# Token windows of 224 instead of 256 in the expert stage, with another order of routing, gap and dense entry, in a fused attention, expert and dense kernel

## The chip, the cores and the metric

The kernel runs on one core of one Trainium2 chip. The metric is the device time of one execution in microseconds (us), the median of three runs. The engines are TensorE (PE; its weight loads stand apart as PEld), VectorE (DVE), ScalarE (ACT), GpSimd (POOL) and SyncE (SP, which issues most DMAs). Each engine works off its own queue in order, and engines wait for one another by semaphores.

## The reference

Three stages on 1,536 tokens, cut to what matters:

```python
# A: attention, B=2, H=8, S=768, D=64; a key is seen only in its query's hash bucket
mask   = q_bucket[:, :, :, None] == k_bucket[:, :, None, :]      # 6 sign bits of x @ proj
attn   = softmax(where(mask, q @ k.T / 8, -1e9))
x      = (attn @ v) as (1536, 512)
# B: one expert of 8 for each token, w1[e] 512x1024, w2[e] 1024x512, capacity 384
expert = argmax(x @ w_gate);  gate_w = softmax(x @ w_gate)[expert]
disp[e, pos] = x[i]           # pos counts the tokens of expert e so far
y      = relu(disp @ w1) @ w2;  out[i] = gate_w[i] * y[expert[i], pos[i]]
# C: dense block, w_in 512x2048, w_out 2048x512
h = out @ w_in;  g = h * clip(h + 3, 0, 6) / 6;  result = g @ w_out
```

With the inputs that the reference draws, the eight experts get 192, 202, 210, 177, 218, 182, 193 and 162 tokens.

## The kernel before

All large products are made of operands that are split in two: a high part that TensorE takes in its faster fp32 form (`fp32r`), and the rest. ACT copies the high part, DVE or Pool subtracts it, and a product takes three matmuls (high by high, low by high, high by low). Weight tiles are `wh` and `wl` (experts), `ia`/`ib` and `ch`/`cl` (dense block); activations are `xh`/`xl`, `hh`/`hl`, `yTh`/`yTl`, `gh`/`gl`.

**Attention (stage A)** runs over 96 steps, one for each chunk of 128 queries of a head. In a step PE makes scores, transposes and the product with v, ACT evicts (`pf`, L398) and takes the high part (`phi`, L406), DVE reduces, and Pool makes the low part (`plo`, L412) of most steps. Work beside the steps (preparing heads, gating, routing) is put into a queue by `at(step, f)` and `spread(step, generator, distance)`, which runs one piece of a generator, up to its next `yield`, every `distance` steps; `due` (called twice a step) issues what has fallen due. The numbers in the table `Q` are such places; `Q['ht']` is a count of dummy matmuls, called heats, which only keep PE busy.

**Routing.** `route(b, ...)` takes the gate logits `lg` of half b of the tokens and finds expert, place in the expert (`pos`) and, by comparing with `edges`, the window in which the token lies. `rh` and `rg` carry token number and gate weight into a matrix of places (`ohr`), and `windows` sums them by matmuls into `ids` (which token stands at a place) and `gates`. `weigh(b)` makes the gate weights. Half 0 is done within the attention; half 1 only after its last step: that stretch, from the last attention step to the first expert product, is called the gap here.

**The gap** goes: rest of `route(1)`, `ids`, `gather(0)` (two indirect DMAs on Pool's queue fetch two tiles `xg` of 128 tokens), the rest of the gate weights, `gates`, `scale_x` (DVE multiplies `xg` by the gate), `make_x` (PE transposes the tiles, ACT and DVE split them into `xh`, `xl`), first `gemm1`. Beside it the first expert's `w1` is split by `split_w(wp, e, i, q, lo)`: tile i of the expert in four quarters q of 512 columns, ACT for `wh` (L131), and DVE or Pool for `wl` (L132). Before the change the four quarters of the first half and three of the second have Pool as `lo`.

**Experts (stage B).** An expert's window of W = 256 tokens is the moving side of all its matmuls, the weights (128 x 128) are the stationary side:

```python
for l, r in ((a, xh), (b, xh), (a, xl)):      # gemm1, 8 tiles of 128 hidden units
    for k in range(KD):                       # KD = 4
        pe.matmul(ps, l[:, c], r[:, k], ...)  # 128x128 weights, W columns
```

`gemm1` (L953) makes 96 matmuls and `gemm2` (L970) makes 96, so eight experts make 1,536. The splits of the next weights, the loads, the next gather and the transposes of its tiles are written between them. The result goes to `yTh`/`yTl` at the expert's offset. During the last expert's second product the dense block's weights begin to be loaded and decoded.

**Overflow.** Tokens of an expert behind the window (W to 384) are done by `rest(e)` under a branch, `If(over > 0)`, which loads the expert's weights once more.

**Dense block (stage C).** The weights come as 64-bit words. `decode` (L999, L1002, L1003) makes fp32 of one 128 x 512 tile in three DVE operations; `split_in` and `halve` split it on ACT (`ia`, `ch`) and Pool (`ib`, `cl`). The loop runs over 32 blocks m (16 groups of hidden units for each half of 768 tokens): `up(m)` makes a group's hidden values (24 matmuls, L1209, in two pieces of 512 and 256 tokens; ACT L1211 and DVE L1212 evict each, then ACT L1221 and DVE L1222 split), and `down(m - 2)` makes 18 matmuls (L1231). `dec_c` decodes the next tile; from m = 2 on it is also called inside `up`, between the two pieces. Behind the branch ten matmuls on `warm_ps` (L1195) come first.

Of the kernel before, what the change touches and what calls it, by code (L numbers as in the profile page):

```python
# [33 lines left out]
W = 256  # L34
CB = 768
NS = NT // P
YW = NT + W
# [12 lines left out]
def moe_attention_kernel(ctx, tc, qk, v, vt, pj, wg, w1, w2, win, wout, out, cap):  # L50
# [27 lines left out]
    edges = persist([P, 4], F32, "edges")  # L78
# [7 lines left out]
    ids = persist([P, E, 3], I32, "ids")  # L86
    gates = persist([P, E, 3], F32, "gates")
# [6 lines left out]
    def consts():  # L94
# [9 lines left out]
        pool.iota(edges, pattern=[[P, 4]], base=0, channel_multiplier=0, **small)  # L104
# [47 lines left out]
    jo = rtile([B, NC, 3], "jo")  # L152
    rh = rtile([B, NC, E, 3], "rh", F16)
    rg = rtile([B, NC, E, 6], "rg", F16)
# [9 lines left out]
    def route(b, psum):  # L164
# [23 lines left out]
        for i in range(b):  # L188
# [7 lines left out]
        ge = rtile([n, 4], f"ge{b}")  # L196
        dve.tensor_tensor(out=ge, in0=bc(pos[:, b], 4), in1=mid(edges, n), op=ALU.is_ge)
        yield
        dve.tensor_tensor(out=t1, in0=ge[:, :, 1], in1=ge[:, :, 2], op=ALU.add)
        dve.tensor_tensor(out=jo[:, b], in0=ge[:, :, 0:3], in1=ge[:, :, 1:4], op=ALU.subtract)  # L200
        yield
        place = rtile([n], f"pl{b}")
        dve.scalar_tensor_tensor(out=place, in0=t1, scalar=-float(P), in1=pos[:, b], op0=ALU.mult, op1=ALU.add)
        jt = rtile([n, 3], f"jt{b}")
        dve.scalar_tensor_tensor(
            out=jt, in0=bc(tokid[:, b * n : (b + 1) * n], 3), scalar=1.0, in1=jo[:, b], op0=ALU.add, op1=ALU.mult
# [4 lines left out]
        for c in range(n):  # L211
            if b and c == n - 1:
                off = rtile([P], "off")
                act.activation(off, iota_r, AF.Square, bias=place[:, c : c + 1], scale=-1.0)
                act.activation(ohr[:, b, c], off, AF.Relu, bias=1.0, scale=-1.0)
                continue
            dve.tensor_scalar(
                out=ohr[:, b, c], in0=iota_r, scalar1=place[:, c : c + 1], scalar2=None, op0=ALU.is_equal
            )

    def weigh(b):
# [13 lines left out]
        jt = rtile([n, 3], f"jg{b}")  # L235
        dve.tensor_tensor(out=jt, in0=jo[:, b], in1=bc(gt[:, b], 3), op=ALU.mult)
        j2 = rtile([n, 6], f"j2{b}", F16)
        dve.tensor_copy(j2[:, :, 0:3], jt)
        yield
        dve.tensor_tensor(out=jt, in0=jt, in1=j2[:, :, 0:3], op=ALU.subtract)  # L240
        dve.tensor_scalar(out=j2[:, :, 3:6], in0=jt, scalar1=LS, scalar2=None, op0=ALU.mult)
# [13 lines left out]
    Q = {'v': (-3.25, -4.75, -1.75, -2.25), 'vg': (-4.5, -4.75), 'vgd': 1, 'pr': (-13.0, -12.75, -12.0, -12.5), 'prd': 0.6, 'b0': 7.75, 'b': 1.75, 'bd': 0.5, 'vm0': (8.0, 8.25, 10.75, 13.0), 'vm': (-0.5, 4.75, 7.0, 12.25), 'vs': 13.25, 'pa': 1.5, 'ev': 0.5, 'lvt': -5.0, 'v4': (2.0, 3.75, 4.0, 16.25), 'vg0': (1.85, -4.4, 7.75), 'p2': 3.5, 'lr': (0, 3, 1.5, 4.5), 'lv': 5.5, 'vsd': 0.75, 'ac': (0, 0, 2, 6, 7, 8, 9, 10), 'hd': (3, 5, 17), 'hn': (4, 4, 2, 2, 4, 3, 0, 0, 0), 'ap': (0,), 'h0': (7,), 'hl': (4,), 'l0': (), 'll': (1, 10), 'ht': (4, 4)}  # L255


    with ExitStack() as actx:
# [524 lines left out]
        for q in range(4):  # L783
            split_w(wp1, 0, 0, q, pool)
# [16 lines left out]
        for _ in range(7):  # L801
            next(rgen)

# [126 lines left out]
    def make_x(e, j):  # L930
# [7 lines left out]
        c = slice(j * P, (j + 1) * P)  # L938
# [95 lines left out]
    dve.tensor_copy(ids, ps1[:, : 3 * E].rearrange("p (e j) -> p e j", e=E))  # L1034
# [9 lines left out]
    ps2 = ps2[:, : 6 * E].rearrange("p (e j) -> p e j", e=E)  # L1044
    dve.tensor_copy(gates, ps2[:, :, 0:3])
    dve.scalar_tensor_tensor(
        out=gates, in0=ps2[:, :, 3:6], scalar=1.0 / LS, in1=gates, op0=ALU.mult, op1=ALU.add
    )
# [74 lines left out]
    with ExitStack() as octx:  # L1123
# [14 lines left out]
        def rest(e):  # L1138
            ra = act.value_load(offs[0:1, E + e : E + e + 1], min_val=0, max_val=NT)
            rv = dve.value_load(offs[0:1, E + e : E + e + 1], min_val=0, max_val=NT)  # L1140
            t = op.tile([P, DM], F32, tag="xo", name=f"xo{e}")
            pool.indirect_dma_start(
                out=t, out_offset=None, in_=xd,
                in_offset=bass.IndirectOffsetOnAxis(ap=ids[:, e, 2:3], axis=0),
            )
            dve.tensor_scalar(out=t, in0=t, scalar1=gates[:, e, 2:3], scalar2=None, op0=ALU.mult)
            ps = pso.tile([P, KD, P], F32, tag="a", name=f"psoa{e}")
            for k in range(KD):
                pe.transpose(ps[:, k], t[:, k * P : (k + 1) * P], ident)
            xo = op.tile([P, KD, P], F32, tag="xt", name=f"xot{e}")  # L1150
            act.activation(xo, ps, AF.Copy)
            ho = op.tile([P, KF, P], F32, tag="ho", name=f"ho{e}")
            for i in range(2):
# [170 lines left out]
```

## Time and profile before

| | us |
|---|---|
| median of three runs | 740.39 |
| the three runs | 734.89, 740.39, 741.52 |
| the profiled execution | 734.49 |
| its span | 732.8 |
| its time outside the span | 1.7 |

| engine | busy us of the span | share |
|---|---|---|
| PE | 695.7 | 95% |
| PEld (weight loads) | 617.5 | 84% |
| DVE | 508.6 | 69% |
| ACT | 383.7 | 52% |
| POOL | 267.1 | 36% |

Matmuls are pipelined and their ends are modelled, so the distance between starts tells what a matmul costs, and not its duration. The granted TensorE clock is given as a share of full speed (2.4 GHz); 0.5 is the lower level (1.2 GHz). The trace shows how the span divides: attention to 228, its last steps and the gap to 259.2, experts to 451.8, the branch to 457.1, and the dense block to the end.

### The profile page before, as it was taken

To read this page: it belongs to the slowest core of one execution; us is meant where nothing else is said; L and a number is where in the kernel's file an instruction comes from. 1 tells how busy PE (TensorE), PEld (TensorE's weight loads), DVE (VectorE), ACT (ScalarE), POOL (GpSimd) and SP (SyncE) were. 2 spreads that over 40 slices of the span, in tenths; PEclk is the share of its full clock that TensorE was granted. 3 is DMA by queue.
4 is the path that set the end of the run, shared out by engine and by line. 5 is a ranking of instruction groups with operands and counts; after the bars stand their busy time and mean duration, and the time that the engine had idled before them with its cause. 6 is when DMAs were issued, how large, how long until landed. Compare 5 with 4: busy or idle time off the path is not lost. (4 is left out here: it accounts for less than half of the span.)

```text
span 732.8 us, 14199 instructions
## 1 busy us (share of the span) xinstructions
PE 695.7 (95%) x5518; PEld 617.5 (84%) x5518; DVE 508.6 (69%) x981; ACT 383.7 (52%) x713; POOL 267.1 (36%) x208
## 2 busy tenths in 40 slices
PE   7999999999889399999999998899999999999996
PEld 2589898899878299999999997788888788888885
DVE  6779888987988867778777777788888732222320
ACT  2468788788769355556555662333333433332320
POOL 4366987887762711100110002333333423221112
PEclk9899999999989789999999999999999999999999
DMA  7576847745460466666666553234433001000001
GB/s 218 135 202 158 241 112 178 229 120 135 127 171 24 125 201 205 194 195 201 198 201 193 172 184 120 82 120 129 129 115 119 27 15 44 30 0 1 1 29 58
DMA packets 37839, 94.14 MB, mean 128 GB/s; under 512 B 7576, under 2 KB 13720, under 8 KB 37760
## 3 DMA queue, kind: packets, MB, share of 16 engines
q1 hardware_dynamic: 34672, 85.71, 39.9%
q0 software_dynamic: 2400, 7.36, 3.0%
q8 instruction: 47, 0.77, 0.4%
q14 instruction: 32, 0.26, 0.1%
q10 hardware_dynamic: 688, 0.03, 0.1%
HBM read 67.14 MB, written 6.29 MB: 100 GB/s over the span
## 5 line engine op out<-in xcount | busy, mean ns | idle before, releaser
L412 POOL TENSOR_TENSOR plo<-pf,phi 128x768 f16<-128x768 f32 x86 | 146.6, 1732 | 62.5 <-ACT phi L406 22.0
L988 POOL TENSOR_TENSOR ib<-wi,ia 128x512 fp32r<-128x512 f32 x32 | 49.1, 1535 | 192.5 <-ACT ia L987 189.4
L382 DVE TENSOR_REDUCE mx<-psm 128x1 f32<-128x384 f32 x192 | 96.4, 549 | 28.2 <-PE psm L379 28.1
L398 ACT ACTIVATE pf<-pst 128x384 f32<-128x384 f32 x192 | 84.1, 488 | 51.5 <-PE pst L397 47.9
L132 DVE TENSOR_TENSOR wl<-raw,wh 128x512 fp32r<-128x512 f32 x121 | 86.4, 724 | 8.1 <-ACT wh L131 2.8
L1209 PE MATMUL psg<-yTh,ia 128*128 128x512 f32 (+1 forms) x256 | 86.9, 339 | 3.5 <-DVE rl L1212 3.1
L1212 DVE SCALAR_TENSOR_TENSOR rl<-rl,psg 128x512 f32<-128x512 f32 x64 | 35.1, 551 | 73.7 <-ACT rl L1211 73.7
L1209 PE MATMUL psg<-yTl,ia 128*128 128x512 f32 (+1 forms) x256 | 86.1, 336 | 0.0
L1209 PE MATMUL psg<-yTh,ib 128*128 128x512 f32 (+1 forms) x256 | 86.1, 336 | 0.0
L1211 ACT ACTIVATE rl<-psg,b 128x512 f32<-128x512 f32 x64 | 37.0, 580 | 84.9 <-PE psg L1209 80.9
L131 ACT ACTIVATE wh<-raw 128x512 fp32r<-128x512 f32 x128 | 77.0, 623 | 2.0 <-issue 2.0
L396 PE MATMUL pst<-Y,K 128*128 128x384 f32 x192 | 75.3, 392 | 0.0
L1231 PE MATMUL pso<-ch,gh 128*128 128x512 f32 x192 | 75.0, 391 | 0.0
L1231 PE MATMUL pso<-ch,gl 128*128 128x512 f32 x192 | 75.0, 391 | 0.0
L1231 PE MATMUL pso<-cl,gh 128*128 128x512 f32 x192 | 74.7, 389 | 0.0
L970 PE MATMUL psy<-hh,wh 128*128 128x256 f32 x256 | 73.7, 288 | 0.0
L406 ACT ACTIVATE phi<-pf 128x768 f16<-128x768 f32 x85 | 71.7, 844 | 2.0
L379 PE MATMUL psm<-K,X 76*128 76x384 f32 x192 | 68.3, 434 | 4.4 <-DVE mx L382 2.2
L970 PE MATMUL psy<-hl,wh 128*128 128x256 f32 x256 | 72.4, 283 | 0.0
L970 PE MATMUL psy<-hh,wl 128*128 128x256 f32 x256 | 72.4, 283 | 0.0
L424 PE MATMUL psv<-vh,phi 128*128 128x73 f16 x576 | 70.2, 200 | 0.0
L425 PE MATMUL psv<-vh,phi 128*128 128x72 f16 x576 | 69.7, 201 | 0.0
(204 smaller groups left out, 1681.0 us busy)
## 6 DMA issues: line engine op xcount, KB each, us to landing
raw<-in_w_dram SPq DMA_DIRECT2D x64, 512.0 KB
rc<-in_win_dram SPq DMA_DIRECT2D x16, 512.0 KB
rc<-in_wout_dram SPq DMA_DIRECT2D x16, 512.0 KB
r<-in_qk_dram SPq DMA_DIRECT2D x16, 384.0 KB
K<-hi SPq DMA_DIRECT2D x31, 192.0 KB
vr<-in_v_dram SPq DMA_DIRECT2D x4, 768.0 KB
vt<-in_vt_dram SPq DMA_DIRECT2D x8, 384.0 KB
Y<-hi SPq DMA_DIRECT2D x16, 192.0 KB
```

Of the source, the lines that this page charges most:

```text
L131: act.activation(wh[e, i][:, c], r, AF.Copy)
L132: lo.tensor_tensor(out=wl[e, i][:, c], in0=r, in1=f32(wh[e, i])[:, c], op=ALU.subtract)
L382: dve.tensor_reduce(out=mm[:, c, n : n + 1], in_=ps[:, :HS], axis=AX.X, op=ALU.max)
L396: pe.matmul(ps[:, :HS], st["K1"][:, kc], st["Y"][:, qc], start=True, stop=False)
L398: act.activation(pf.rearrange("k (c n p) -> k c n p", c=NC, n=2)[:, :, n], ps[:, :HS].rearrange("k (p c) -> k c p", c=NC), AF.Exp, scale=0 ...
L406: act.activation(phi_t[k], pf_t[k], AF.Copy)
L412: eng.tensor_tensor(out=plo_t[k], in0=pf_t.pop(k), in1=phi_t[k], op=ALU.subtract)
L424: pe.matmul(o, hi[:, cc], vv[:, j, 0:VA], start=j == 0 and c == 0, stop=False, **grp)
L425: pe.matmul(o[:, 0:DE], hi[:, cc], vv[:, j, VA:VW], start=False, stop=False, **grp)
L970: pe.matmul(ps, l, r, start=n == 0, stop=n == 3 * KF - 1)
L1209: pe.matmul(ps, l, x, start=n == 0, stop=n == 3 * KD - 1)
L1231: pe.matmul(po[blk][s], l, r, start=first and n == 0, stop=last and n == 2)
```

## The change

1. **Width.** A window is GW = 112 tokens instead of 128, so W = 224 instead of 256, and there are NW = 4 windows up to the capacity instead of 3. `edges`, `jo`, `rh`, `rg`, `ids` and `gates` grow accordingly, and `rest` loops over two windows. Gathers and transposes still take 128 tokens; `make_x` evicts 112 columns.
2. **Routing.** `route` has a further `yield` after `rs`, and one ahead of each column for half 0; it begins at step 66 with a distance of 1.5 (before: 70 and 1), `weigh(0)` at 84 (before: 88). One more piece of `route(1)` is issued ahead of the gap's code.
3. **Gap.** The first half of the first `w1` is split within attention steps 88.5 to 94.5, by ACT and DVE. Of the second half two quarters are split ahead of `scale_x` and two behind `make_x`, by DVE. Pool makes none of them. The loads of the first `w2` are issued behind `make_x`. Heats: 2 new ones, then 5 and 9 in place of 4 and 4.
4. **Dense entry.** `warm_ps` is allocated ahead of the branch from the pool `pso` that is open there, with 12 matmuls instead of 10. From m = 1 on, the loop issues `up(m)` first, then `split_in(m + 2)` and `dec_c`.

```diff
-W = 256
+GW = 112
+W = 2 * GW
+NW = 4
@@ route
+        yield
         ps = psum()
...
-        dve.tensor_tensor(out=t1, in0=ge[:, :, 1], in1=ge[:, :, 2], op=ALU.add)
+        dve.tensor_reduce(out=t1, in_=ge[:, :, 1:NW], axis=AX.X, op=ALU.add)
...
         for c in range(n):
+            if not b:
+                yield
@@ attention
-        spread(70, route(0, lambda: misc("psr0")))
-        spread(88, weigh(0))
+        spread(66, route(0, lambda: misc("psr0")), 1.5)
+        spread(84, weigh(0))
         for i in range(4):
             at(NC * (NH - 3) + i, load_w, 0, i // 2, i % 2)
+            at(STEPS - 7.5 + 2 * i, split_w, wp1, 0, 0, i)
@@ end of attention
-        for q in range(4):
-            split_w(wp1, 0, 0, q, pool)
...
-        for _ in range(7):
+        for _ in range(8):
             next(rgen)
+        heat(ps_t, "t", 2)
@@ make_x
-        c = slice(j * P, (j + 1) * P)
+        c = slice(j * GW, (j + 1) * GW)
+        ps = ps[:, :, 0:GW]
@@ gap
     gather(0)
     heat(HT[0])
-    for q in range(3):
-        split_w(wp1, 0, 1, q, pool)
     run(wgen)
-    for q in range(4):
-        load_w(0, 2 + q // 2, q % 2)
     windows(ps2, ohr, rg, [B - 1])
...
-    split_w(wp1, 0, 1, 3)
+    split_w(wp1, 0, 1, 0)
+    split_w(wp1, 0, 1, 1)
     for j in range(2):
         scale_x(0, j)
     for j in range(2):
         make_x(0, j)
+    for q in range(2, 4):
+        split_w(wp1, 0, 1, q)
+    for q in range(4):
+        load_w(0, 2 + q // 2, q % 2)
@@ ahead of the branch / dense entry
+        warm_ps = pso.tile([P, 512], F32, tag="w", name="warm_ps", bufs=1)
         with tc.If(over > 0):
...
+        for _ in range(12):
+            pe.matmul(warm_ps, ident16, mid(ident16, 4), start=True, stop=True)
...
-        warm_ps = ps_g.tile([P, 512], F32, tag="g", name="warm_ps")
-        for _ in range(10):
-            pe.matmul(warm_ps, ident16, mid(ident16, 4), start=True, stop=True)
@@ dense loop
-            if m + 2 < TOT:
-                split_in(m + 2)
-            dec_c()
+            if m == 0:
+                split_in(2)
+                dec_c()
             if m < TOT:
                 up(m)
+            if 0 < m < TOT - 2:
+                split_in(m + 2)
+            if m > 0:
+                dec_c()
```

**DVE in the gap, around the gates.** Each row is an instruction: line, operation, written tile, read tiles, shape; numbers behind a name are buffer numbers, `wl0_1` is the second half of the first expert's w1. Before:

```order
L1046 SCALAR_TENSOR_TENSOR gates_77<-psg_4973,gates_77 128x24
L132 TENSOR_TENSOR wl0_1_5022<-raw0_1_1_3895,wh0_1_5021 128x512
L928 TENSOR_SCALAR xg00_5013<-xg00_5013,gates_77 128x512
L928 TENSOR_SCALAR xg01_5015<-xg01_5015,gates_77 128x512
L940 TENSOR_TENSOR xl0_5065<-psa00_5066,xh0_5064 128x4x128
```

DVE had one `wl` here, behind the gates; Pool made the three other quarters. The same place after:

```order
L1049 SCALAR_TENSOR_TENSOR gates_77<-psg_4977,gates_77 128x32
L135 TENSOR_TENSOR wl0_1_5055<-raw0_1_0_3849,wh0_1_5054 128x512 x2
L934 TENSOR_SCALAR xg00_5017<-xg00_5017,gates_77 128x512
L934 TENSOR_SCALAR xg01_5019<-xg01_5019,gates_77 128x512
L947 TENSOR_TENSOR xl0_5063<-psa00_5064,xh0_5062 128x4x112
L947 TENSOR_TENSOR xl0_5063<-psa01_5071,xh0_5062 128x4x112
L135 TENSOR_TENSOR wl0_1_5055<-raw0_1_1_3890,wh0_1_5054 128x512 x2
```

All four quarters stand on DVE now, two ahead of the scalings and two behind the evictions of the transposes.

**ACT in the last attention steps.** `wh_0` is the first expert's w1. Before, the copies of its first half follow the last step (the first of the two rows of four):

```order
L398 ACTIVATE pf_4406<-pst_4407 128x6x64
L398 ACTIVATE pf_4406<-pst_4411 128x6x64
L406 ACTIVATE phi_4435<-pf_4406 128x768
L131 ACTIVATE wh_0_4514<-raw_0_0_3761 128x512 x2
L131 ACTIVATE wh_0_4514<-raw_0_1_3809 128x512 x2
```

After, they stand among the steps; this is the last of them:

```order
L404 ACTIVATE pf_4382<-pst_4383 128x6x64
L404 ACTIVATE pf_4382<-pst_4387 128x6x64
L134 ACTIVATE wh_0_4196<-raw_0_1_3808 128x512
L412 ACTIVATE phi_4415<-pf_4382 128x768
```

One copy stands ahead of a step's `phi`, and nothing but the step's own work is left behind the last one.

**DVE at the dense entry, from the end of block 0 on.** `rl1` and `gl1` are block 1's evictions, `wi4` is the decoding of tile 4. Before:

```order
L1222 TENSOR_TENSOR gl0_9151<-rl0_9119,gh0_9150 128x768
L999 TENSOR_SCALAR wi4_9162<-rc4_0_7705 128x512
L1002 SCALAR_TENSOR_TENSOR wi4_9162<-rc4_0_7705,wi4_9162 128x512
L1003 SCALAR_TENSOR_TENSOR wi4_9162<-rc4_0_7705,wi4_9162 128x512
L1212 SCALAR_TENSOR_TENSOR rl1_9168<-rl1_9168,psg10_9169 128x512
L1212 SCALAR_TENSOR_TENSOR rl1_9168<-rl1_9168,psg11_9184 128x256
```

After:

```order
L1233 TENSOR_TENSOR gl0_10051<-rl0_10019,gh0_10050 128x768
L1223 SCALAR_TENSOR_TENSOR rl1_10054<-rl1_10054,psg10_10055 128x512
L1223 SCALAR_TENSOR_TENSOR rl1_10054<-rl1_10054,psg11_10070 128x256
L1233 TENSOR_TENSOR gl1_10086<-rl1_10054,gh1_10085 128x768
L1006 TENSOR_SCALAR wi4_10097<-rc4_0_7715 128x512
L1009 SCALAR_TENSOR_TENSOR wi4_10097<-rc4_0_7715,wi4_10097 128x512
```

The decoding moved behind block 1's evictions.

## Rows read from the trace of the kernel before

**Rows 1.** Windows: stretch, length, busy us (count) by engine, granted clock, DMA share, GB/s.

```profile
0.00:228.00 228.00, 215.45 (x2307) 184.39 (x2308) 188.09 (x431) 164.01 (x296) 156.85 (x122) 0.96 0.61 163
228.00:259.20 31.20, 19.07 (x254) 13.79 (x252) 25.50 (x64) 18.12 (x39) 16.92 (x15) 0.83 0.34 106
259.20:451.80 192.60, 192.58 (x1606) 192.05 (x1606) 148.09 (x301) 109.32 (x231) 14.33 (x14) 0.99 0.60 187
457.10:580.00 122.90, 119.62 (x608) 101.47 (x608) 105.42 (x128) 44.74 (x74) 41.90 (x29) 1.00 0.34 107
```

**Rows 2.** Waits of PE from 225 to 560: total us, times, longest.

```profile
PE psa L937 <- DVE xg L928: 4.2, 1, 4.2
PE warm_ps L1195 <- ACTq L1176: 3.0, 1, 3.0
PE psg L1209 <- DVE rl L1212: 2.7, 1, 2.7
```

**Rows 3.** Timeline of PE: start, us, operation, written<-read, stationary, output, count.

```profile
52.46 1.49 PE L485 MATMUL psg<-wg_sb,vt 128*128 128x16 f32 x12
53.79 0.43 PE L396 MATMUL pst<-Y,K 128*128 128x384 f32 x1
```

**Rows 4.** Weight loads by line: busy us, mean ns, idle time before them.

```profile
L970 PEld LDWEIGHTS psy<-hh,wl 128*128 128x128 f32 x256 | 49.0, 191 | 0.0
...
L485 PEld LDWEIGHTS psg<-wg_sb,vt 128*128 128x128 f32 x96 | 11.9, 198 | 0.0
```

**Rows 5.** Windows as in rows 1, three short stretches.

```profile
229.50:238.50 9.00, 8.97 (x148) 7.42 (x147) 7.65 (x19) 8.84 (x17) 1.55 (x1) 1.00 0.02 4
259.20:262.00 2.80, 2.80 (x13) 2.71 (x14) 1.33 (x2) 0.45 (x1) 1.25 (x2) 0.50 0.94 287
442.30:452.50 10.20, 9.48 (x80) 9.28 (x78) 9.93 (x16) 2.81 (x6) 3.61 (x2) 1.00 0.43 129
```

**Rows 6.** Timeline of ACT at the end of the attention, columns as in rows 3.

```profile
238.41 2.17 ACT L131 ACTIVATE wh<-raw 128x512 fp32r<-128x512 f32 x4
```

**Rows 7.** Timeline of POOL in the gap.

```profile
239.86 4.93 POOL L132 TENSOR_TENSOR wl<-raw,wh 128x512 fp32r<-128x512 f32 x4
250.83 0.97 POOL L921 DMA_INDIRECT xg<-xd,ids  x1 [0.30 <-DVE rg L160]
251.81 3.71 POOL L132 TENSOR_TENSOR wl<-raw,wh 128x512 fp32r<-128x512 f32 x3
```

**Rows 8.** Timeline of DVE in the gap.

```profile
241.36 1.05 DVE L461 TENSOR_TENSOR lg<-xp,lg 128x48 f32<-128x48 f32 x1
242.68 0.95 DVE L172 TENSOR_TENSOR dl<-lg,mx 128x48 f32<-128x48 f32 x1
243.66 1.19 DVE L175 SCALAR_TENSOR_TENSOR sc<-dl,rank 128x48 f32<-128x48 f32 x1
245.12 0.21 DVE L180 TENSOR_TENSOR oh<-sc,mx 128x48 f16<-128x48 f32 x1
...
251.31 4.77 DVE L132 TENSOR_TENSOR wl<-raw,wh 128x512 fp32r<-128x512 f32 x1
256.00 0.87 DVE L928 TENSOR_SCALAR xg<-xg,gates 128x512 f32<-128x512 f32 x2
259.77 0.76 DVE L132 TENSOR_TENSOR wl<-raw,wh 128x512 fp32r<-128x512 f32 x1
```

**Rows 9.** Transfers of the gathered tiles, 240 to 300, from the view of that tile.

```profile
DMA to landing us min/median/max: 3.3/4.1/6.1
```

**Rows 10.** The chain that ended last: start, us, engine, tile, line.

```profile
464.07 1.44 DVE wi L999
465.53 1.65 DVE wi L1002
...
579.24 0.42 DVE rl L1212
...
581.40 4.11 PE pso L1231 x18
```

More of the change, by code (lines that the diff above doesn't have):

```diff
@@ L33 @@
 KG = DF // P
-W = 256
+GW = 112
+W = 2 * GW
+NW = 4
 CB = 768
 NS = NT // P
-YW = NT + W
+YW = NT + 2 * P
 DE = D + E
@@ L85, in moe_attention_kernel @@
     lg = persist([P, B, NC, E], F32, "lg")
-    ids = persist([P, E, 3], I32, "ids")
-    gates = persist([P, E, 3], F32, "gates")
+    ids = persist([P, E, NW], I32, "ids")
+    gates = persist([P, E, NW], F32, "gates")
     inv = persist([P, NS], I32, "inv")
@@ L103, in consts @@
         pool.iota(iota_r, pattern=[[1, P]], base=0, channel_multiplier=0, **small)
-        pool.iota(edges, pattern=[[P, 4]], base=0, channel_multiplier=0, **small)
+        pool.iota(edges, pattern=[[GW, NW + 1]], base=0, channel_multiplier=0, **small)
+        pool.memset(edges[:, NW:], float(cap))
         pool.iota(iota_s, pattern=[[1, NS]], base=0, channel_multiplier=0, **small)
@@ L233, in weigh @@
         yield
[L235 to L238, printed above, removed]
+        jt = rtile([n, NW], f"jg{b}")
+        dve.tensor_tensor(out=jt, in0=jo[:, b], in1=bc(gt[:, b], NW), op=ALU.mult)
+        j2 = rtile([n, 2 * NW], f"j2{b}", F16)
+        dve.tensor_copy(j2[:, :, 0:NW], jt)
         yield
-        dve.tensor_tensor(out=jt, in0=jt, in1=j2[:, :, 0:3], op=ALU.subtract)
-        dve.tensor_scalar(out=j2[:, :, 3:6], in0=jt, scalar1=LS, scalar2=None, op0=ALU.mult)
+        dve.tensor_tensor(out=jt, in0=jt, in1=j2[:, :, 0:NW], op=ALU.subtract)
+        dve.tensor_scalar(out=j2[:, :, NW:], in0=jt, scalar1=LS, scalar2=None, op0=ALU.mult)
         yield
@@ L1033, in moe_attention_kernel @@
     windows(ps1, ohr, rh, [B - 1])
-    dve.tensor_copy(ids, ps1[:, : 3 * E].rearrange("p (e j) -> p e j", e=E))
+    dve.tensor_copy(ids, ps1[:, : NW * E].rearrange("p (e j) -> p e j", e=E))
     gather(0)
     heat(HT[0])
-    for q in range(3):
-        split_w(wp1, 0, 1, q, pool)
     run(wgen)
-    for q in range(4):
-        load_w(0, 2 + q // 2, q % 2)
     windows(ps2, ohr, rg, [B - 1])
     heat(HT[1])
-    ps2 = ps2[:, : 6 * E].rearrange("p (e j) -> p e j", e=E)
-    dve.tensor_copy(gates, ps2[:, :, 0:3])
+    ps2 = ps2[:, : 2 * NW * E].rearrange("p (e j) -> p e j", e=E)
+    dve.tensor_copy(gates, ps2[:, :, 0:NW])
     dve.scalar_tensor_tensor(
-        out=gates, in0=ps2[:, :, 3:6], scalar=1.0 / LS, in1=gates, op0=ALU.mult, op1=ALU.add
+        out=gates, in0=ps2[:, :, NW:], scalar=1.0 / LS, in1=gates, op0=ALU.mult, op1=ALU.add
     )
-    split_w(wp1, 0, 1, 3)
+    split_w(wp1, 0, 1, 0)
+    split_w(wp1, 0, 1, 1)
     for j in range(2):
@@ L1140, in rest @@
             rv = dve.value_load(offs[0:1, E + e : E + e + 1], min_val=0, max_val=NT)
[L1141 to L1153, printed above, removed]
-                r = op.tile([P, 2048], F32, tag="wo", name=f"wo{e}{i}", bufs=2)
-                sp.dma_start(out=r, in_=w1[e, :, i * 2048 : (i + 1) * 2048])
-                for f in range(4):
-                    ps = pso.tile([P, P], F32, tag="h", name=f"psoh{e}{i}{f}")
-                    for k in range(KD):
-                        pe.matmul(
-                            ps, r[:, k * 512 + f * P : k * 512 + (f + 1) * P], xo[:, k],
-                            start=k == 0, stop=k == KD - 1,
-                        )
-                    act.activation(ho[:, 4 * i + f], ps, AF.Relu)
```

69 lines of the change are left out of this document (47 added, 22 removed).

## The prediction

> **What bounds the kernel now.** I read the windows by stage first. In the attention TensorE is busy for 215.45 of 228 us, in the expert stage for 192.58 of 192.60 us at a granted clock of 0.99, and in the first half of the dense block for 119.62 of 122.9 us [rows 1]. Only the stretch from 228 to 259.2 us is different: 19.07 of 31.2 us, at 0.83. So a change that makes matmuls shorter is worth its full amount in the expert stage, and a change in the order of instructions is worth something only in the gap and at the dense block's entry, where TensorE waits. Next I read TensorE's waits from 225 to 560 us [rows 2]: 4.2 us for the scaled tiles `xg`, 3.0 us of `warm_ps` for ACT, 2.7 us for a dense eviction on DVE. These waits and the clock are all that parts 2 to 4 of the change can win. The sum below is made against the profiled execution: 734.49 us, a span of 732.8 and 1.7 outside. That execution lies 5.9 us under the median of 740.39; two runs lie at 734.5 to 734.9, two at 740.4 to 741.5. A measurement of this kernel can therefore hardly tell 1% (7.4 us) from no change.
>
> **The width: −13.0 us (bounds 0 and −19.4).** In the expert stage 1,606 matmuls take 192.58 us [rows 1], which is 119.9 ns each; 1,536 of them are the expert products, 184 us. What would a matmul of 224 columns take? Two things can pace it. One is the columns. A dense matmul of 512 columns takes 4.11 / 18 = 228 ns [rows 10], one of 256 takes 120, so a column costs (228 − 120) / 256 = 0.42 ns, and 224 columns would take 120 − 32 × 0.42 = 106.5 ns. The other is the load of its 128 x 128 fp32 weights, which every product needs anew and which the width doesn't shorten. The nearest row for that are the gate matmuls: they have only 16 columns, with loads of the same form, and twelve of them take from 52.46 to 53.79 us [rows 3], 111 ns each. Their loads last 198 ns in the mean, and the experts' 191 [rows 4], so a load of split weights is not seen to be slower than theirs. I take 111 ns: 9 ns gained on each. The bounds are 106.5 ns (the columns, were the load quicker than in the gate) and 120 ns (no row excludes that the experts' loads already pace their matmuls). The last expert's second product, 96 matmuls, is left out of the count, because there DVE is busy for 9.93 of 10.2 us with evictions and four decodings [rows 5] and sets the end. So 1,440 × 9 ns = 13.0 us, and 1,440 × 13.5 = 19.4 at most.
>
> The Trainium skill (TensorE: Matmul & The Clock Gate, section LDWEIGHTS) speaks against the hope that width pays in full: it gives a load as its columns divided by 1.2 GHz, whatever the contraction, so an estimate from that page is 107 ns for 128 columns and a gain of 13 ns each, 18.7 us in all. By the gate's 111 ns the trace agrees within 4 ns; no row has these products under 256 columns.
>
> Other work is no new bound there: DVE has 148.09 and ACT 109.32 us of 192.6 [rows 1], their evictions get shorter with the width, and the DMA share of 0.60 would rise to 0.64 in 179 us. The wider `ids`, `gates` and `rh` and the new places of `route(0)` and `weigh(0)` I count at zero: in the attention DVE has 40 us free [rows 1], and 0.5 us either way changes no bound.
>
> **The gap: −4.2 us (bounds −0.4 and −6.9).** Four terms.
>
> (a) The four `wh` copies of the first half take 2.17 us together [rows 6]. They move from behind the last step into the last steps, where ACT is busy for 8.84 of 9.0 us and TensorE for 8.97 [rows 5]. ACT has no room, so I count +2.2. DVE gets the four `wl` too, 0.76 each [rows 8], in the same nine steps with 7.65 of 9.0 busy: 1.35 us of room for 3.0. If both paced one after another it would be +5.1. If a backlog on ACT were taken up by the distance between the steps, 0.
>
> (b) Pool works from 239.86 to 244.79 on its four `wl` [rows 7], and just then three small DVE operations take 1.05, 0.95 and 1.19 us [rows 8], where the next one of the same size takes 0.21 when Pool has finished. They stand on the path from logits to `ids`. Without Pool: −2.5. Four DVE `wl` no longer stand here, since they are in the steps.
>
> (c) DVE's `wl` behind the gates starts at 251.31 and takes 4.77 us, alone 0.76 [rows 8]; it ends when Pool's three `wl` (251.81 to 255.52 [rows 7]) end. `scale_x` starts only then, and its end at 256.87 releases the transposes, TensorE's wait of 4.2 us [rows 2]. With two `wl` on DVE and none on Pool, DVE is free at about 252.9, and what comes last is the second gather: issued at 250.83 [rows 7], landed 3.3 us later at best [rows 9], at 254.1. Its scaling then ends at 254.6: −2.2. The first tile is scaled and transposed by then, and its four transposes at the low clock go from the path: −0.8.
>
> The Trainium skill (SBUF — State Buffer, in its rule on the shared port pair of VectorE and GpSimd) says that the loser of an exclusive lock waits for one whole instruction of the other. The row differs: 4.77 us is not one Pool operation of 1.24 (3.71 / 3) but all three. By the page's rule the `wl` would have cost about 2.0, and the gain of (c) would be 2.2 all the same, since the gather sets it.
>
> (d) The first 2.8 us of the expert stage run at a granted clock of 0.50, with 13 matmuls [rows 5], 0.215 us each instead of 0.111: 1.35 us lost. The heats that become more (16 instead of 8) and the shorter wait can keep the clock up; I count 0.9 of it, with 0 and 1.35 as the ends.
>
> Sum: +2.2 − 2.5 − 3.0 − 0.9 = −4.2. With (a) at 5.1 and (d) at 0 it is −0.4, with (a) at 0 and (d) at 1.35 it is −6.9. The loads of `w2`, now behind `make_x`, wait for tiles that the splits set free in any case, and the first `gemm2` is a whole `gemm1` (over 10 us) away.
>
> **The dense entry: −1.4 us (bounds 0 and −3.2).** `warm_ps` waits for ACT because its PSUM space is that of the experts' tiles; in the new pool it waits for its own engine alone. The wait of 3.0 us [rows 2] goes, but the first real product needs the decoded and split weights, and DVE ends its last eviction with four decodings almost without a pause [rows 5]; what is left is a product that no longer stands behind two late warm matmuls, −0.5. The wait of 2.7 us at block 2 [rows 2] comes from the decoding, 1.44 and 1.65 us for its first two operations of three, that stands ahead of block 1's evictions on DVE [rows 10]. Behind them it holds up nobody at once, and the wait goes. But the decoding isn't saved: DVE is busy for 105.42 of 122.9 us up to 580 [rows 1] in a chain that ends with the eviction at 579.24 [rows 10], and the decoding that was put off is put behind later evictions there. I count −0.9 of the 2.7, since some of DVE's idle 17 us takes it up, with 0 and −2.7 as the ends.
>
> **The sum.** −13.0 − 4.2 − 1.4 = −18.6, so 715.9 us beside 734.49. Half of the runs lie 6 us over the profiled one, so I add 2: **718 us**.
>
> **The rivals.** R1: the weight loads of the split products already pace them at 120 ns. For it: their weight loads never pause (idle 0.0 [rows 4]). Against it: the gate's loads are as long and follow one another in 111 ns. Only parts 2 to 4 are left: 734.5 − 5.6 = 728.9. Chance 0.13.
>
> R2: the end of the attention takes the place of the gap. ACT and DVE pace the last steps by the full 5.1 us, and the wait in the gap keeps the clock low: (a) at 5.1, (d) at 0, the gap gives 0.4, the sum 719.7 beside the profile. Against it: DVE has 1.35 us free there. Chance 0.12.
>
> R3, slower: narrow products lose the fast fp32 form and run in two passes like plain fp32. The gate shows such passes: 48 products leave 96 loads [rows 4], 111 ns each, 222 ns a product. Then each expert product costs 222 instead of 120 ns, 1,536 × 0.102 = 157 us, and the time would be about 890; it decides as soon as a product of 224 columns takes more than 120 ns + 5.6 / 1,536 us = 124 ns. Every product of this form in the trace has 256 columns or more, so nothing speaks against it but that no row shows a penalty. Chance 0.07.
>
> R4, slower: an expert with more than 224 tokens sends the kernel into `rest`, which now loads 4 MB of weights for each of two windows, at the stage's 187 GB/s [rows 1] 22 us each, some 45 us for one expert: 760. It decides from 225 tokens; the largest expert has 218. Chance 0.02.
>
> **How the numbers follow.** The forecast has 0.66, R1 0.13, R2 0.12, R3 0.07, R4 0.02. The range has to hold the forecast with its bounds and most of R1 and R2: the lower end is the columns' 106.5 ns with the rest as counted (715.9 − 6.4 = 709.5) less a little of the gap's bound, 708; the upper end is R1's 728.9 with the 2 for the runs, 731. R3 and R4, some of R1 and the corner of all lower bounds (705) stay out. Faster by over 1% means under 733.0: the forecast, R2 and most of R1, 0.84; within 1%: the rest of R1, 0.07; slower 0.09.
>
> **What would show it.** The expert stage takes 179 to 180 us with TensorE busy throughout, its matmuls 111 ns apart; at 120 it is R1, over 200 R3. In the gap the DVE operations on logits take 0.2 us, `scale_x` waits for a DMA and not for `wl`, and the first expert products run at the full clock or not. The last attention steps take about 2 us longer. At the dense entry the two waits of 3.0 and 2.7 us are gone, and the time up to the first second-half block falls by less than they. The forecast fails if the matmuls do not follow the column count down to 111, or if TensorE waits in the expert stage for a load or split that the shorter products overtake.

## The result, and the profile after

The changed kernel takes 715.88 us (median of four runs, 714.69 to 717.72), the kernel before 738.03 beside it (four runs, 734.89 to 741.52): a ratio of 0.967, 95% interval 0.963 to 0.971. The profiled execution has a span of 713.0 us, 19.8 less than before. The time lies 2 us from the forecast, but the terms of the sum do not all lie so near.

The windows of the changed kernel, cut at the same events as the table below: steps 72 to 88 of the attention, from there to its last product, the gap, the first and the second expert, and all experts. Columns: stretch, length, busy us (count) of PE, PEld, DVE, ACT, POOL, granted clock, DMA share, GB/s.

```profile
184.67:219.82 35.15, 33.13 (x408) 30.25 (x405) 31.93 (x74) 28.30 (x52) 26.58 (x18) 1.00 0.56 156
219.82:239.53 19.71, 15.58 (x254) 13.14 (x252) 17.93 (x40) 14.45 (x28) 3.45 (x3) 0.98 0.08 23
239.53:253.67 14.14, 9.06 (x60) 4.35 (x58) 9.36 (x39) 4.45 (x14) 6.06 (x7) 0.67 0.62 200
253.67:276.21 22.54, 22.54 (x202) 22.52 (x203) 19.02 (x51) 14.44 (x31) 2.50 (x3) 1.00 0.71 229
276.21:298.52 22.31, 22.31 (x202) 22.31 (x201) 18.25 (x43) 13.78 (x30) 1.90 (x3) 1.00 0.65 212
253.67:431.95 178.28, 178.28 (x1605) 178.09 (x1606) 144.32 (x302) 106.89 (x233) 13.59 (x13) 1.00 0.61 203
```

The same cuts in the kernel before (its rows 1 have other cuts), up to the second expert:

```profile
184.39:224.75 40.36, 35.42 (x408) 32.21 (x405) 35.22 (x81) 27.99 (x51) 26.23 (x18) 0.92 0.51 136
224.75:240.33 15.58, 15.12 (x255) 12.71 (x252) 13.48 (x32) 15.23 (x30) 4.25 (x4) 1.00 0.10 29
240.33:259.19 18.86, 7.19 (x54) 4.00 (x50) 15.16 (x38) 5.97 (x17) 13.53 (x13) 0.71 0.51 157
259.19:284.60 25.41, 25.41 (x202) 25.32 (x203) 18.63 (x48) 13.79 (x29) 3.15 (x4) 0.94 0.63 199
284.60:308.50 23.90, 23.90 (x203) 23.90 (x202) 18.57 (x42) 14.24 (x30) 1.89 (x2) 1.00 0.62 198
```

All stages, in us. The last three lines are read from the starts of the first and last products in the two timelines.

| stretch | before | after | difference | forecast |
|---|---|---|---|---|
| to step 72 | 184.4 | 184.7 | +0.3 | 0 |
| steps 72 to 88 | 40.4 | 35.2 | −5.2 | 0 |
| step 88 to the last attention product | 15.6 | 19.7 | +4.1 | +2.2 |
| gap | 18.9 | 14.1 | −4.7 | −5.5 |
| experts | 192.3 | 178.3 | −14.0 | −13.9 |
| branch | 5.2 | 4.9 | −0.4 | −0.5 |
| first half of the dense block | 128.6 | 128.0 | −0.6 | −0.9 |
| second half, to the end | 147.4 | 148.1 | +0.7 | 0 |

TensorE's waits from 220 to 560 us (total us, times, longest). The three waits of [rows 2] are gone or smaller; what is left of `warm_ps` is for TensorE's own sequencer (PEq). The largest is a new one, at the end of the attention. [rows 2] leaves out the longest wait of that view before, 5.0 us of the gap's routing products for DVE's `oh`; they wait 2.4 us now (the row names ACT's `ex`).

```profile
PE psr L187 <- DVE oh L180: 5.0, 1, 5.0
```

After:

```profile
PE psv L432 <- DVE plo L418: 2.7, 2, 2.3
PE psr L191 <- ACT ex L231: 2.4, 1, 2.4
PE warm_ps L1195 <- PEq L1187: 1.7, 1, 1.7
PE psa L943 <- DVE xg L934: 1.4, 2, 1.0
...
PE psg L1220 <- DVE rl L1223: 0.2, 1, 0.2
```

The timeline of DVE from the attention's end to the first expert (start, us, operation; in brackets idle time and releaser), to be read beside [rows 8]:

```profile
234.10 2.13 DVE L135 TENSOR_TENSOR wl<-raw,wh 128x512 fp32r<-128x512 f32 x1
236.16 0.27 DVE L223 TENSOR_SCALAR ohr<-iota_r,pl 128x128 f16<-128x128 f16 x1
236.35 1.81 DVE L418 TENSOR_TENSOR plo<-pf,phi 128x768 f16<-128x768 f32 x2
...
240.63 0.21 DVE L467 TENSOR_TENSOR lg<-xp,lg 128x48 f32<-128x48 f32 x1
241.11 0.21 DVE L175 TENSOR_TENSOR dl<-lg,mx 128x48 f32<-128x48 f32 x1
241.35 0.21 DVE L178 SCALAR_TENSOR_TENSOR sc<-dl,rank 128x48 f32<-128x48 f32 x1
...
248.33 1.28 DVE L135 TENSOR_TENSOR wl<-raw,wh 128x512 fp32r<-128x512 f32 x2
250.24 0.49 DVE L934 TENSOR_SCALAR xg<-xg,gates 128x512 f32<-128x512 f32 x1 [0.62 <-DMA xg<-xd,ids]
251.78 0.49 DVE L934 TENSOR_SCALAR xg<-xg,gates 128x512 f32<-128x512 f32 x1 [1.05 <-DMA xg<-xd,ids]
```

The three operations on the logits take 0.21 us each instead of about 1, the two `wl` 1.28 together instead of 4.77 for one, and both scalings wait for a gather. That is what terms (b) and (c) said. The first row is the other side: a `wl` that was moved into the attention stands on DVE ahead of the last `plo`, and takes 2.13 us.

The attention's early part differs between executions of every kernel here: its steps up to the 24th took 62.1 us in the changed kernel's profile and 68.7 in that of one experiment with the same code there (from the first product of each step). So a few us of a total can be that, and below the stretches are compared beside the totals.

### The profile page after: what moved, and what is told of

Read it like the earlier page. It is cut to its first block, busy times and chain, and to the rows that moved or that the text cites. A ratio compares the mean times of both kernels' runs of the same rounds, so it can differ in the third digit from the quotient of the medians.

```text
span 713.0 us, 14233 instructions
## 1 busy us (share of the span) xinstructions
PE 685.0 (96%) x5528; PEld 600.3 (84%) x5528; DVE 504.5 (71%) x988; ACT 379.4 (53%) x713; POOL 260.7 (37%) x202
## 5 line engine op out<-in xcount | busy, mean ns | idle before, releaser
L135 DVE TENSOR_TENSOR wl<-raw,wh 128x512 fp32r<-128x512 f32 x128 | 88.1, 699 | 10.1 <-ACT wh L134 3.7
L1222 ACT ACTIVATE rl<-psg,b 128x512 f32<-128x512 f32 x64 | 37.2, 581 | 94.5 <-PE psg L1220 94.5
L1223 DVE SCALAR_TENSOR_TENSOR rl<-rl,psg 128x512 f32<-128x512 f32 x64 | 35.2, 551 | 73.5 <-ACT rl L1222 73.5
L1242 PE MATMUL pso<-cl,gh 128*128 128x512 f32 x192 | 76.6, 399 | 0.5 <-POOL cl L995 0.5
L977 PE MATMUL psy<-hh,wh 128*128 128x224 f32 x256 | 71.4, 279 | 0.0
L432 PE MATMUL psv<-vh,plo 128*128 128x73 f16 x576 | 68.5, 196 | 2.7 <-DVE plo L418 2.7
L977 PE MATMUL psy<-hl,wh 128*128 128x224 f32 x256 | 70.4, 275 | 0.0
L977 PE MATMUL psy<-hh,wl 128*128 128x224 f32 x256 | 69.9, 273 | 0.0
```

Source lines behind the costliest of these rows:

```text
L135: lo.tensor_tensor(out=wl[e, i][:, c], in0=r, in1=f32(wh[e, i])[:, c], op=ALU.subtract)
L977: pe.matmul(ps, l, r, start=n == 0, stop=n == 3 * KF - 1)
L1242: pe.matmul(po[blk][s], l, r, start=first and n == 0, stop=last and n == 2)
```

## The experiments

The theory that they test: TensorE sets the time from step 72 to the end, so each wait, low clock or ns per matmul that the change removes there counts in full, and parts that move work onto DVE take some of it back. The rivals stand with each run.

**The width alone.** The kernel before with edit 1 (`GW = 112`, four windows, longer tables) and nothing else.

```diff
-W = 256
+GW = 112
+W = 2 * GW
+NW = 4
```

> The kernel before with windows of 224 (two of 112) and nothing else of the change. My theory: the width alone brings 14 us, since TensorE is never idle in the expert stage; first expert product to last 192.3 -> 178 to 179 us, products 112 ns apart instead of 120; gap and dense entry as before; ratio to before 0.980 to 0.984. Rival: the shorter products overtake splits or loads where Pool still has its part, and the stage stays above 185 us. For the dense block: if the 64 bytes by which the longer tables move all later tiles slow its matmuls, the blocks of its second half take 8.30 us instead of 8.26 here too; if the new order of the dense loop does it, they take 8.26.

730.15 us, ratio 0.984 (0.980 to 0.987). Windows of its first expert, its second, and the stretch between experts and dense block:

```profile
263.17:288.73 25.56, 25.56 (x203) 25.49 (x203) 18.01 (x49) 13.38 (x29) 3.57 (x4) 0.88 0.61 194
288.73:311.03 22.30, 22.30 (x202) 22.30 (x201) 18.25 (x43) 13.80 (x30) 1.88 (x3) 1.00 0.70 212
...
444.90:452.55 7.65, 3.87 (x11) 1.49 (x11) 3.86 (x6) 0.92 (x2) 1.26 (x1) 0.64 0.43 142
```

The seven experts behind the first take what they take in the changed kernel, 22.3 us for most. The first takes 3.0 us more than there, at a granted clock of 0.88, and `warm_ps` waits for 4.0 us at the branch, where the clock then is 0.64. The stage takes 181.3 us, 2 to 3 more than expected, and the branch 8.1 against 5.2 in the kernel before. So the width brings its gain per matmul by itself, but about 6 us of its 14 (3.0 and 2.9) are lost at both ends of the stage when the rest of the change is missing.

**The width undone.** The changed kernel with `GW = 128`, `NW = 3`.

> The changed kernel with windows of 256 again (two of 128, three in all), all else kept. My theory: only the width is lost: products 120 ns apart, expert stage 192, gap as in the changed kernel (14.1 us from the last attention product to the first expert product), so about 715.9 + 14 = 730, ratio to before 0.987 to 0.993. Rival: the gap gains only because of the narrower windows, and the time is 734 or more. The tables are as long as before here: dense blocks of the second half at 8.26 us speak for the place of the tiles, at 8.30 for the order of the loop.

730.97 us, ratio 0.985 (0.983 to 0.986), a little better than expected. The expert stage takes 191.1 us against 178.3, products are 120 ns apart again, and the gap stays short at 13.7 us. 12.8 us belong to the width. The two halves of the change together (ratios 0.984 and 0.985) make the whole.

**Narrower still.** The changed kernel with `GW = 96`, so W = 192; four experts have more tokens and take the overflow path too.

> The changed kernel with windows of 192 tokens (two of 96), so that four experts with more tokens run the overflow path too. Only the pace of the products in the expert stage is asked for. My theory: the load of the weights paces them from 224 columns down, so they stay 111 to 112 ns apart and the expert stage at 178 us. Rival: the columns still pace them at 224, and at 192 they are about 98 ns apart, the stage about 157 us. The overflow path loads 4 MB for each of two windows of four experts, so the total is some 180 us or more above the changed kernel.

One run, 963.04 us. The second expert:

```profile
276.15:298.44 22.29, 22.29 (x203) 22.29 (x201) 18.08 (x42) 13.38 (x30) 1.90 (x3) 1.00 0.69 217
```

22.29 us with 192 columns and 22.31 with 224: the products are 111.7 ns apart (`gemm1`, mean of the starts) in both. At 224 columns the columns no longer pace them; 32 less bring nothing. Nor is it a fixed cost of every product: the f16 products of the attention (73 columns, each with a 128 x 128 load of 0.1 us) follow one another at 35 ns in the changed kernel's trace. What is left is the load of the fp32 weights, 192 ns long there and 194 in the gate. The Trainium skill (TensorE: Matmul & The Clock Gate, section LDWEIGHTS) has a formula from which the load is 107 ns by estimate; the runs show 111.7. The overflow path took 253 us for four experts, 63 us each.

**The yield behind `rs`.** The changed kernel without it (and so with one piece less of `route(1)` issued ahead of the gap, which keeps the same code there).

```diff
             dve.tensor_reduce(out=rs[:, b], ...)
-        yield
         ps = psum()
```

> The changed kernel without the new yield behind rs in route, so that TensorE's routing products are issued right behind the DVE operation that they need. My theory: that one yield removed TensorE's wait of 2.5 us for rs in the middle of the attention, so the wait is back and steps 72 to 88 take 37.5 to 38 instead of 35.2 us, the total 2 to 3 us more than the changed kernel. Rival: the wait comes from the earlier place of the routing (66 instead of 70, distance 1.5), and nothing changes.

Steps 72 to 88 take 37.76 us, as expected, with TensorE's wait for `rs` back at 1.5 us. Total 721.84, ratio 0.976 (0.969 to 0.983); 5.1 us of its profiled execution lie ahead of step 24, where the code is the same. The waits of the kernel before in that stretch, 184 to 225 us, had it as their first row; the view of [rows 2] began at 225 and missed it:

```profile
PE psr L190 <- DVE rs L183: 2.5, 1, 2.5
```

and without the yield:

```profile
PE psr L193 <- DVE rs L186: 1.5, 1, 1.5
```

In program order the routing products stand right behind the DVE reduction that they read. TensorE takes its queue in order, so the next step's scores wait behind them for as long as DVE is behind. Since the pieces of `route(0)` come 1.5 steps apart, the yield puts 1.5 steps between the two.

**All places of the routing.** As above, and `route` at 70 with distance 1, `weigh` at 88, no yields per column.

> The changed kernel with all of the routing's places of before: no new yields, route at 70 with distance 1, weigh at 88. My theory: the whole gain of 5.2 us in steps 72 to 88 goes (they take 40 instead of 35.2 us), with the half clock back around step 84; total 4 to 6 us more than the changed kernel. Rival: the half clock there comes from elsewhere, and only the 2.5 us of the wait for rs come back.

Steps 72 to 88 take 41.68 us at a clock of 0.88:

```profile
187.82:229.50 41.68, 36.28 (x407) 33.41 (x404) 35.28 (x81) 27.96 (x51) 26.21 (x18) 0.88 0.47 131
```

Total 723.95, ratio 0.979 (0.972 to 0.986). The 5.2 us are gone, and 1.3 more. In the kernel before, the window from 215 to 220 us has a granted clock of 0.50, and 31 matmuls; in the changed kernel it has 1.00, and 68.

```profile
215.00:220.00 5.00, 4.44 (x31) 3.43 (x31) 3.67 (x12) 2.57 (x6) 0.00 (x0) 0.50 0.00 0
```

Groups of four steps keep the two parts apart. Steps 72 to 76 take 8.1 us in the changed kernel, 11.1 without the yield and 10.7 with the old places; steps 84 to 88 take 9.4, 9.4 and 13.3. So the routing's order is worth 5 to 6 us: 2.6 for one yield, the rest for the other places, and part of that by the clock. Which of the other places does it (`route`, `weigh` or the columns) was not separated.

**The first four splits behind the attention again.**

```diff
-            at(STEPS - 7.5 + 2 * i, split_w, wp1, 0, 0, i)
...
         tally(NH // 2 - 1, pool, (0,))
+        for q in range(4):
+            split_w(wp1, 0, 0, q, pool)
```

> The changed kernel with the first four splits behind the attention again, ACT and Pool. My theory: the last steps (88 to the end of the attention) win back 4 us, 1.4 in the steps and 2.7 in TensorE's wait for a plo that stands on DVE behind the splits, and the DVE operations on the logits lose 2.5 us to Pool again, so the total is 1 to 2 us lower than the changed kernel or the same. Rival: the splits behind the attention hold up more than the logits, and the time is 2 us or more longer.

From step 88 to the last product, and the gap:

```profile
220.29:236.80 16.51, 15.03 (x256) 12.71 (x252) 14.89 (x36) 14.88 (x28) 4.73 (x4) 1.00 0.10 27
236.80:253.15 16.35, 9.07 (x62) 4.34 (x58) 11.97 (x39) 4.56 (x14) 10.29 (x11) 0.69 0.54 163
```

The attention's end is 3.2 us shorter and the gap 2.2 us longer; together 1.0 us better than the changed kernel. With the changed kernel's code the two take 33.1 to 34.7 us in the profiles here, and about 32.9 with this edit, alone or among the three below. 715.37 us, ratio 0.968 (0.961 to 0.975): no difference that a total can show. The operations on the logits are as slow as before the change (1.05, 0.95 and 1.19 us), beside Pool's `wl` as in [rows 8]; the second of them:

```profile
239.15 0.95 DVE L175 TENSOR_TENSOR dl<-lg,mx 128x48 f32<-128x48 f32 x1
```

So this part of the change moved its cost from one place to the other.

**The old heats.** `'ht': (4, 4)`, and no `heat(ps_t, "t", 2)`.

> The changed kernel with the heats of before: 4 and 4, none at the end of the attention. My theory: the heats are what lets the first expert run at the full clock, so here it takes 24 to 25.5 us instead of 22.5, and the total is 1.5 to 3 us longer. Rival: the shorter wait for the gathered tiles alone does it, the first expert stays at 22.5 us and the time is the same within 1 us.

The first expert:

```profile
253.84:278.46 24.62, 24.62 (x202) 24.55 (x203) 19.21 (x51) 14.43 (x31) 2.43 (x3) 0.91 0.66 208
```

The gap is as long as with the new heats (14.2 us), but the first expert runs at a granted clock of 0.91 in the mean and takes 2.1 us more; the second takes 22.31 us at 1.00. Total 719.22, ratio 0.974 (0.967 to 0.982). The heats and not the shorter wait give the clock.

**The old order of the dense loop.**

```diff
-            if m == 0:
-                split_in(2)
-                dec_c()
+            if m + 2 < TOT:
+                split_in(m + 2)
+            dec_c()
             if m < TOT:
                 up(m)
-            if 0 < m < TOT - 2:
-                split_in(m + 2)
-            if m > 0:
-                dec_c()
```

> The changed kernel with the dense loop's order of before (split_in, dec_c, up). My theory: the new order wins 1.9 us up to block 3 and gives it back, since each block of the first half waits about 0.1 us for cl from Pool (blocks of 8.45 instead of 8.26 us, twelve of them, 2.3 us); so here the entry to block 3 takes 20.2 instead of 18.3 us, the later blocks of the first half 8.3 and the total moves by less than 1 us. Rival: the new order is a plain gain, the blocks stay at 8.45 here, and the time is 2 us longer.

From block 0 to block 3 it takes 20.17 us instead of 18.30, and the blocks after it 8.36 instead of 8.45 (mean of blocks 4 to 13). Up to the second half it is 128.69 against 127.99: the new order is worth 0.7 us. 721.37 us, ratio 0.975 (0.971 to 0.979), with single runs from 716.3 to 726.9; its profiled execution has a span of 714.6, and no stretch of it shows the rest of that total.

**`cl` ahead of `ib`.** In the changed kernel TensorE starts `down` while Pool has only just made `cl`. The timeline of Pool, and of PE, in one block:

```profile
482.07 1.55 POOL L995 TENSOR_TENSOR ib<-wi,ia 128x512 fp32r<-128x512 f32 x1 [5.47 <-ACT ia L994]
483.58 1.47 POOL L995 TENSOR_TENSOR cl<-dt,ch 128x512 fp32r<-128x512 f32 x1
```

```profile
484.90 0.40 PE L1242 MATMUL pso<-ch,gl 128*128 128x512 f32 x1
485.13 0.47 PE L1242 MATMUL pso<-cl,gh 128*128 128x512 f32 x1
485.44 0.39 PE L1242 MATMUL pso<-ch,gh 128*128 128x512 f32 x1
```

`cl` ends at 485.05; behind the product with it the next comes 0.31 us later, where 0.23 is usual. The edit puts `dec_c()` ahead of `split_in(m + 2)` for m > 0, so that `cl` is made first.

> The changed kernel with dec_c ahead of split_in in the dense loop, so that Pool makes cl before ib. My theory: TensorE's wait of 0.1 us in each block of the first half is for cl behind ib on Pool, so the blocks go from 8.45 to 8.36 us (what the old order had at this place of the tiles), 1 us or a little more in all, with the short entry kept (18.3 us to block 3). Rival: DVE or ACT sets the blocks, and they stay at 8.45.

The blocks take 8.38 us instead of 8.45, block 3 comes at 17.57 instead of 18.30, and the first half takes 127.28 instead of 127.99. Total 716.17, ratio 0.968 (0.962 to 0.975): 0.7 us by the profile, which a total cannot show.

**64 and 192 unused bytes behind the constants.** `ids`, `gates` and `edges` are longer in the changed kernel, and every tile allocated behind them from that end of the memory (`yTh`, `yTl`, `gh`, `gl`, half of the `ch`, `cl`) lies 64 bytes further, while those from the other end (`ia`, `ib`) stay.

```diff
-    b3 = persist([P, 1], F32, "b3")
+    b3 = persist([P, 17], F32, "b3")[:, 0:1]
```

and `[P, 49]` in the second run; the tiles then lie 128 and 256 bytes from their old places.

> The changed kernel with 64 unused bytes behind the constants, so that all tiles behind them lie 128 bytes and not 64 from their old places. Theory of the place: the 512-wide dense matmuls go from 230 back to 226.5 ns, the blocks of the second half from 8.30 to 8.26, 0.6 to 2 us in all. Rival: the place does not matter, 8.30 stays and the time is the same.

> The changed kernel with 192 unused bytes behind the constants, so that the tiles behind them lie 256 bytes from their old places. The run with 64 bytes showed that the place matters, and that 128 is no better than 64. Theory: what matters is where the tiles lie within 256 bytes against those at the other end of the memory; then the blocks of the dense block's second half take 8.26 us again (8.32 in the changed kernel, 8.39 with 64), its 512-wide matmuls 226.7 to 228.2 ns, and the total is about 1 us less. Rival: any distance from the old place costs, and the blocks stay at 8.3 or more.

A block of the second half in the three kernels (the chain that ended last: start, us, product). The changed kernel:

```profile
585.63 4.20 PE pso L1242 x18
589.84 4.12 PE psg L1220 x24
```

with 64 bytes more:

```profile
586.14 4.20 PE pso L1242 x18
590.33 4.22 PE psg L1220 x24
```

with 192 bytes more:

```profile
586.28 4.11 PE pso L1242 x18
590.38 4.15 PE psg L1220 x24
```

The kernel before has 8.26 us for a block there, like the last. The means over blocks 16 to 26 are 8.26 (before), 8.32 (64 bytes off), 8.39 (128) and 8.26 (256); with windows of 256 and the tables' old length 8.26 too, and with the width alone, which has the longer tables and the old loop, 8.32. The theory of the place holds as the second run put it: 128 bytes were worse and 256 as good as the old place. Totals: 717.68 (ratio 0.968, 0.966 to 0.969) and 717.34 (0.971, 0.964 to 0.979); the effect of 1 to 2 us is seen in the blocks alone.

**Three edits together.** 192 bytes, `cl` first, and the first four splits behind the attention.

> The changed kernel with three edits together: 192 unused bytes behind the constants, dec_c ahead of split_in, and the first four splits behind the attention as before. My theory: blocks of 8.26 us in both halves (0.9 and 2.3 us), 1 us at the end of the attention: 3 to 4 us less than the changed kernel, ratio to before 0.962 to 0.966. Rival: the dense block's first half has another bound at 8.4, and 1 to 2 us are left.

714.70 us, ratio 0.967 (0.961 to 0.974), a span of 711.2 against 713.0: less than expected, as the rival had it. The second half is at 8.27 a block. In the first, blocks 3 to 5 take 8.26, but from block 6 on they creep to 8.4 to 8.5, and TensorE waits for `cl` again: in this block the product with it starts 0.32 us behind the one before, and the next 0.34 behind it.

```profile
491.36 0.40 PE L1243 MATMUL pso<-ch,gl 128*128 128x512 f32 x1
491.68 0.50 PE L1243 MATMUL pso<-cl,gh 128*128 128x512 f32 x1
492.02 0.40 PE L1243 MATMUL pso<-ch,gh 128*128 128x512 f32 x1
```

The bound of about 8.45 us is DVE, by the traces. Its round of a block (evictions, six decoding operations and `gl`) has one pause, 0.9 us, for ACT's `gh`, and that in turn waits for DVE's `rl`; it waits for neither TensorE nor Pool (but two of its operations are slow beside Pool, see the end). The starts of `gl`, one a block, are 8.45 us apart in this run from block 1 to block 13, and equally in the kernel before and the changed one. Before, then after:

```profile
503.54 0.96 DVE L1222 TENSOR_TENSOR gl<-rl,gh 128x768 fp32r<-128x768 f32 x1 [0.91 <-ACT gh L1221]
512.00 0.96 DVE L1222 TENSOR_TENSOR gl<-rl,gh 128x768 fp32r<-128x768 f32 x1 [0.91 <-ACT gh L1221]
```

```profile
506.88 0.96 DVE L1233 TENSOR_TENSOR gl<-rl,gh 128x768 fp32r<-128x768 f32 x1 [0.91 <-ACT gh L1232]
515.35 0.96 DVE L1233 TENSOR_TENSOR gl<-rl,gh 128x768 fp32r<-128x768 f32 x1 [0.91 <-ACT gh L1232]
```

Where TensorE's blocks take 8.26 us, DVE falls behind by 0.19 in each, until TensorE waits: in the kernel before, blocks 14 and 15 (counted from 0) take 8.80 and 8.74 us. With `cl` first (8.41 us in most blocks) block 15 takes 8.99. The order of the loop thus chooses at which block TensorE pays, more than how much: the first half takes 127.2 to 128.7 us in all of these.

## Why the prediction was right, step by step

**The width** held in mechanism and size. 111 ns from the gate's rows was the pace (111.7 measured), and 12.8 us the gain (13.0 forecast). R1 (120 ns) and R3 (two passes) are out: products of 224 and of 192 columns run in one pass at the pace of the load. That the load and not the columns bounds them was a choice between bounds in the prediction; the run with 192 shows it. Two small errors cancel in the size: a product gained 8.3 ns and not 9, and the last expert's second product, left out because DVE was to set its end, gained as much as the others (the last expert takes 21.3 us instead of 22.9).

**The gap** held: −4.7 against −5.5 for (b) and (c), with the rows that were named. From the last attention product to the end of `gates` it takes 8.9 us instead of 11.1, so (b) is −2.2; putting Pool's first four `wl` back brings the slow operations and 2.2 us of gap back. From there to the first expert product it takes 5.3 instead of 7.8, so (c) is −2.5 against −3.0: the second scaling ends 3.9 us behind the gates (5.5 before), since its gather, as forecast, comes last. No run puts (c) back alone; it rests on these rows. (d) was forecast as −0.9 and is −1.3: the first expert is 2.9 us shorter, of which 1.6 is the width (23.90 to 22.31 in the second). The old heats show that the new ones do it.

**Term (a) was right on ACT and missed DVE.** It took ACT for the engine without room (+2.2). Over the whole stretch ACT is busy for 14.45 of 19.71 us and DVE for 17.93, but up to 235 us both are nearly full:

```profile
219.82:235.00 15.18, 13.37 (x203) 10.95 (x200) 14.76 (x37) 14.10 (x28) 2.07 (x2) 1.00 0.10 28
```

The copies do delay ACT: its last `phi` starts 14.7 us behind the start of step 88 (219.82), and 13.4 us in the run with the splits behind the attention (220.29). First the changed kernel, then that run:

```profile
234.51 0.84 ACT L412 ACTIVATE phi<-pf 128x768 f16<-128x768 f32 x1
```

```profile
233.65 0.84 ACT L412 ACTIVATE phi<-pf 128x768 f16<-128x768 f32 x1
```

These are 1.3 of the 3.2 us that this run wins at the attention's end. The other 1.9 are DVE's: of its four `wl`, one overlaps Pool's `plo` and takes 2.13 us instead of 0.7; the last two `plo` then stand behind it on DVE, and TensorE waits 2.7 us for them. The step that failed is the 1.35 us of room that a mean over nine steps gave to DVE. The whole loss is 4.1 us, between the forecast and R2's upper end (5.1; by its own rows 2.17 and four times 0.76 are 5.2). R2, with both engines, gave the rest right too, that the gap's gain is then nearly eaten: from step 88 to the first expert product the change wins 0.6 us (34.4 to 33.9). Its second condition, a low clock after it, did not come, thanks to the heats.

**The routing was forecast as nothing and won 5.2 us.** That is the largest miss. The step that failed is "I count at zero: in the attention DVE has 40 us free". DVE's busy share over 228 us says nothing on the moment at which TensorE's queue stands behind one DVE result. The evidence was there, a wait of 2.5 us and a stretch at half the clock before 225 us, but the waits were read from 225 on. Two runs show that the gain comes from the routing's places. It happens to pay for what the other terms fell short by, about 4 us for (a), the gap and the dense block together, and so the sum came out right: beyond the width and the gap, the closeness of the total is luck.

**The dense entry** was forecast as −1.4 and is −0.3 with what follows it. The wait for the eviction went; that for `warm_ps` fell from 3.0 to 1.7 us. The branch took 4.8 to 6.9 us in the runs with the new entry, so its 0.4 us are not shown. The new order alone is worth 0.7 us against the old one at the same place, near the 0.9 counted. The prediction's reason (the decoding is put off, not saved) holds: DVE's round of 8.45 us is the same in both kernels. What the sum lacked is the place of the tiles: 0.06 us a block in the second half, some 0.7 to 0.9 us, from tables that grew by 64 bytes.

R4 could not happen with these inputs; its price was too low (45 us an expert against 63 in the run with 192).

## What to carry to other kernels

Before narrowing the moving side of a matmul, look for a matmul in the same trace that is bound by the weight load: here its pace was the floor, and the columns from 192 to 224 cost nothing. An instruction on the bounding engine's queue that reads a fresh result of another engine holds up everything behind it, so put other work between producer and consumer, and read the waits over the whole span and not only around the edit that looks large. Work that is moved out of a gap goes somewhere: ask which queue it then stands on, and who waits behind it there. Where one engine waits now and then for another, measure the other's own round: an order of instructions can move the wait, but the longer round sets the time.

## What was not expected of the hardware

The place of tiles in the memory changes the pace of matmuls. The 512-wide dense products take 226.7 ns (`up`) and 228.2 (`down`) with the tiles at their old place or 256 bytes from it, 229.8 and about 232 at 64 bytes, 232.4 and about 232 at 128, in the same stretch of the second half, as means of the distance of starts. The 256-wide ones take 119.3, 116.0 and 119.6 at 0, 64 and 128 bytes. Why is open: only the shift of one end's tiles against the other's was tried.

A DVE operation with two operands in SBUF can be held up by a Pool operation that it meets: here once by a single one (2.13 us instead of 0.7). The Trainium skill (SBUF — State Buffer, rule on the shared port pair) says that the loser waits for one whole instruction; this row agrees, while the 4.77 us of [rows 8] were three.

This also bears on the engine that sets the dense block's first half. In each of the changed kernel's blocks two of DVE's six decoding operations take 1.52 and 1.67 us beside Pool's `ib` and `cl`; the same two on the other tile take 0.42 and 0.69. No run took Pool's two operations away.
